# Strassen-like products in the first layer of the last two experts of a balanced mixture, on one core

## The chip, the cores and the metric

The kernel runs on one core of a Trainium2 chip. A core has a matrix engine (TensorE, PE in the profile; its weight loads are shown as PEld), a vector engine (VectorE, DVE), a scalar engine (ScalarE, ACT), a general engine (GpSimd, POOL) and a synchronising engine that starts transfers (SyncE, SP). The metric is the time of one execution on the device in microseconds (us), as the median of several runs.

## What is computed

A linear attention (RWKV-5) over 4 batches, 8 heads, 768 steps and a head dimension of 48 gives 3072 rows of 384 channels. These go through a mixture of 8 experts, which each take exactly 384 tokens, chosen by sorted gate values:

```python
def _moe_ref(x, w_gate, w1, w2) -> np.ndarray:        # N, D, E, F = 3072, 384, 8, 1024
    cap = N // E                                      # 384 tokens of each expert
    logits = x @ w_gate
    ...                                               # greedy, balanced assignment of tokens to experts
    for e in range(E):
        mask = assigned == e
        h = np.maximum(x[mask] @ w1[e], 0.0)          # first layer: 384 x 384 by 384 x 1024
        out[mask] = h @ w2[e]                         # second layer: 384 x 1024 by 1024 x 384
```

Everything is float32. The change concerns the line of the first layer, for the two experts that the kernel takes last.

## The kernel before

The experts are taken one after the other, n = 0 to 7. For each of them the kernel knows the 384 tokens by then, has gathered their rows into `xg` and loaded the weights; it turns the rows to `xT` (channels on the partitions), computes the first layer into `hid`, and the second layer into the output's rows. Constants: `KD = 3` blocks of 128 channels, `KF = 8` blocks of 128 hidden units, `CAP = 384` tokens, `NC = 3` blocks of 128 tokens, `HF = 4`, `HX = 192`.

The first layer is straight: eight blocks of hidden units by three blocks of channels, so 24 matmuls of 384 columns.

```python
    def products(h_ps, j, w1, xT, cols=slice(0, CAP)):
        for f in range(KD):
            product = nc.tensor.matmul(h_ps[:, cols], w1[:, f, ts(j, 128)], xT[:, f, cols],
                                       start=(f == 0), stop=(f == KD - 1))
        return product.ins

    def hidden(hid, j, w1, xT):
        h_ps = ps_h.tile([128, CAP], F32, name="h_ps")
        product = products(h_ps, j, w1, xT)
        nc.scalar.activation(hid[:, j, :], h_ps, AF.Relu)
        return product
```

The second layer is straight for the last block of 128 tokens (`result`, 8 matmuls of 384 columns). For the first two blocks together (`results`) it already uses seven products of sums of quarters instead of eight: the quarters of `hid` (two blocks of tokens by two halves of the hidden units) and of `w2` (two halves of the hidden units by two halves of the channels). The sums are made on VectorE, of `w2` in `halves_of`, of `hid` in `S`:

```python
    def halves_of(w2):
        B = [[w2[:, ts(i, HF), ts(j, HX)] for j in range(2)] for i in range(2)]
        T = [tpool.tile([128, HF, HX], F32, name=f"T{i}") for i in range(4)]
        for t, a, b in ((0, B[0][1], B[0][0]), (1, B[1][1], T[0]), (2, B[1][1], B[0][1]), (3, B[1][0], T[1])):
            nc.vector.tensor_sub(T[t], a, b)
        return B, T

    def results(n, hid, weights, tok, turn):
        B, T = weights
        A = [[hid[:, ts(k, HF), ts(c, 128)] for k in range(2)] for c in range(2)]
        S = ...                                       # 4 sums of 128 x 512 on VectorE
        ...
        p1, p6 = pair((A[0][0], B[0][0]), (S[1], T[1]))     # a pair: 2 x 4 matmuls of 192 columns
        one = spool.tile([128, HX], F32, name="one")
        nc.scalar.copy(one, p1)
        both = sum_of(p6, one, "both")
        p7, p5 = pair((S[2], T[2]), (S[0], T[0]))
        low = sum_of(p7, both, "low")
        nc.vector.tensor_add(out[1][:, HX:DX], p5, low)
        high = sum_of(p5, both, "high")
        xT = turn()                                   # transposes of the next expert's rows
        p2, p4 = pair((A[0][1], B[1][0]), (A[1][1], T[3]))
        ...
        p3, = pair((S[3], B[1][1]))
        nc.vector.tensor_add(out[0][:, HX:DX], p3, high)
        store(n, 0, out[0], tok)
        return xT, added[-1]
```

The loop: while one expert is computed, `following` finds the next expert's tokens and starts the loads of its weights. For most experts that is a search with matmuls and many small VectorE operations; for the last expert only the remaining tokens have to be listed (`walk.remainder`).

```python
        else:                                         # n = 1 to 7
            ...
                weights_2 = halves_of(at["w2"])
            walk.behind = hidden(hid, 0, at["w1"], xT)
            if n + 1 < E:
                ahead = following(n + 2 == E)
            for j in range(1, KF):
                hidden(hid, j, at["w1"], xT)
            for _ in result(n, 2, hid, at["w2"], at["tok"]):
                pass
        xT, added = results(n, hid, weights_2, at["tok"], lambda: turn(ahead["xg"]) if n + 1 < E else None)
```

The accumulators lie in PSUM: two buffers `h_ps`, two buffers `o_ps` and two for transposes, each in a bank of its own. `w1`, `w2`, `T`, `S` and the sums have two buffers each. The order of instructions on each engine isn't that of the text: a scheduler lays it out by the order of the text and by when it reckons that operands are ready, so that a later operation may be put into a gap ahead of an earlier one.

Of the kernel before, what the change touches and what calls it, by code (L numbers as in the profile page):

```python
# [11 lines left out]
F32 = mybir.dt.float32  # L12
# [4 lines left out]
AF = mybir.ActivationFunctionType  # L17
# [5 lines left out]
T = 128  # L23
# [1161 lines left out]
def rwkv5_eagle_then_base_layer_balanced(  # L1185
# [12 lines left out]
    nc = tc.nc  # L1198
    N, DX = out.shape
    E, _, F = moe_w1.shape  # L1200
    NT = N // 128
    CAP = N // E
    NC = CAP // 128
    KD = DX // 128
    KF = F // 128
# [10 lines left out]
    def ask(number, w1, cols=slice(0, F)):  # L1216

        def by(fmax):
            nc.vector.tensor_scalar(out=number, in0=fmax[0:1, :], scalar1=-1.0, scalar2=float(E),
                                    op0=ALU.mult, op1=ALU.add)  # L1220
            weights(number, w1, cols, nc.sync)
        return by
# [8 lines left out]
    def fetch(xg):  # L1231
        def rows(tok):
            for c in range(NC):
                nc.gpsimd.indirect_dma_start(  # L1234
                    out=xg[:, c, :], out_offset=None, in_=x_dram,
                    in_offset=bass.IndirectOffsetOnAxis(ap=tok[:, c:c + 1], axis=0))
        return rows
# [4 lines left out]
    xg = once.tile([128, NC, DX], F32, name="xg")  # L1242
    w1 = once.tile([128, KD, F], F32, name="w1")
    ahead = dict(walk.slots(), number=number, w1=w1, xg=xg)
# [29 lines left out]
    spool = ctx.enter_context(tc.tile_pool(name="f_s", bufs=2))  # L1274
    opool = ctx.enter_context(tc.tile_pool(name="f_o", bufs=3))
    ps_t = ctx.enter_context(tc.tile_pool(name="f_ps_t", bufs=2, space=PSUM))
    ps_h = ctx.enter_context(tc.tile_pool(name="f_ps_h", bufs=2, space=PSUM))
    ps_o = ctx.enter_context(tc.tile_pool(name="f_ps_o", bufs=2, space=PSUM))

    def second(at, queue):  # L1280
        if "w2" not in at:
            at["w2"] = wpool.tile([128, KF, DX], F32, name="w2")
        w2 = at["w2"]
        queue.dma_start(w2, moe_w2[which(at["number"], queue)].rearrange("o (c p) d -> p (o c) d", p=128))

    def following(last, pieces=None, late=None):
        at = dict(walk.slots(), number=xpool.tile([1, 1], I32, name="number"),
                  w1=wpool.tile([128, KD, F], F32, name="w1"), xg=xpool.tile([128, NC, DX], F32, name="xg"))
        make = at, ask(at["number"], at["w1"]), fetch(at["xg"])
        if last:  # L1290
            walk.remainder(*make)
        else:
            if pieces:

                def between(most):
                    for _ in range(most):
                        next(pieces, None)

                with tc.manual_schedule(engines={nc.tensor.engine}):
                    next(pieces)  # L1300
                    walk.between = between
                    listed = walk.search(at)
                    walk.between = Assignment.between
                    for _ in pieces:
                        pass
                with tc.issue_after(listed):
                    late()
            else:
                walk.search(at)
            walk.settle(*make)  # L1310
        second(at, nc.sync)
        return at

    def turn_rows(xT, xg, c):
        xT_ps = ps_t.tile([128, KD, 128], F32, name="xT_ps")
        for f in range(KD):
            nc.tensor.transpose(xT_ps[:, f, :], xg[:, c, ts(f, 128)], ident)  # L1317
        return nc.scalar.copy(xT[:, :, ts(c, 128)], xT_ps).ins  # L1318

    def turn(xg):  # L1320
        xT = xpool.tile([128, KD, CAP], F32, name="xT")
        for c in range(NC):
            turn_rows(xT, xg, c)
        return xT
# [7 lines left out]
# [5 lines that stand above are left out]
# [27 lines left out]
            nc.scalar.activation(hid[:, j, :], h_ps, AF.Relu)  # L1364
            yield

    HF, HX = KF // 2, DX // 2

    def halves_of(w2):

# [6 lines that stand above are left out]
    def store(n, c, o_sb, tok):  # L1377
        nc.gpsimd.indirect_dma_start(  # L1378
            out=out_rows[n * NC + c], out_offset=bass.IndirectOffsetOnAxis(ap=tok[:, c:c + 1], axis=0),
            in_=o_sb, in_offset=None)  # L1380

    def result(n, c, hid, w2, tok):

        o_ps = ps_o.tile([128, DX], F32, name="o_ps")
        for j in range(KF):
            nc.tensor.matmul(o_ps, hid[:, j, ts(c, 128)], w2[:, j, :], start=(j == 0), stop=(j == KF - 1))  # L1386
            yield
        o_sb = opool.tile([128, DX], F32, name="o_sb")
        nc.scalar.copy(o_sb, o_ps)
        store(n, c, o_sb, tok)  # L1390
# [5 lines that stand above are left out]
        S = [spool.tile([128, HF, 128], F32, name=f"S{i}") for i in range(4)]  # L1396
        nc.vector.tensor_sub(S[2], A[0][0], A[1][0])
        nc.vector.tensor_add(S[0], A[1][0], A[1][1])
        nc.vector.tensor_sub(S[1], S[0], A[0][0])
        nc.vector.tensor_sub(S[3], A[0][1], S[1])  # L1400

        def pair(*factors):
            o_ps = ps_o.tile([128, DX], F32, name="o_ps")
            parts = [o_ps[:, ts(i, HX)] for i in range(len(factors))]
            for part, (a, b) in zip(parts, factors):
                for j in range(HF):
                    nc.tensor.matmul(part, a[:, j, :], b[:, j, :], start=(j == 0), stop=(j == HF - 1))  # L1407
            return parts

        def sum_of(product, other, name):  # L1410
            out = spool.tile([128, HX], F32, name=name)
            added.append(nc.vector.tensor_add(out, product, other).ins)  # L1412
            return out

        added = []
        out = [opool.tile([128, DX], F32, name="o_sb") for _ in range(2)]
        p1, p6 = pair((A[0][0], B[0][0]), (S[1], T[1]))
# [7 lines that stand above are left out]
        xT = turn()  # L1425
        p2, p4 = pair((A[0][1], B[1][0]), (A[1][1], T[3]))
        nc.vector.tensor_add(out[1][:, 0:HX], p4, low)  # L1427
        store(n, 1, out[1], tok)
        nc.vector.tensor_add(out[0][:, 0:HX], p2, one)  # L1429
# [5 lines that stand above are left out]
    for n in range(E):  # L1435
        at = ahead
        hid = hpool.tile([128, KF, CAP], F32, name="hid")
        if n == 0:
            xT = xpool.tile([128, KD, CAP], F32, name="xT")
            at["w2"] = wpool.tile([128, KF, DX], F32, name="w2")  # L1440
            weights_2 = []

            def late():
                weights_2[:] = halves_of(at["w2"])

            ahead = following(n + 2 == E, chain(opening(hid, at, xT), result(n, 2, hid, at["w2"], at["tok"])), late)
        else:
            with ExitStack() as order:
                if n == 1:

                    order.enter_context(tc.issue_after(added))
                weights_2 = halves_of(at["w2"])
            walk.behind = hidden(hid, 0, at["w1"], xT)
            if n + 1 < E:
                ahead = following(n + 2 == E)
            for j in range(1, KF):
                hidden(hid, j, at["w1"], xT)
            for _ in result(n, 2, hid, at["w2"], at["tok"]):
                pass
        xT, added = results(n, hid, weights_2, at["tok"], lambda: turn(ahead["xg"]) if n + 1 < E else None)  # L1460


# [26 lines left out]
```

## Time and profile before

| | before |
|---|---|
| time, median of 3 runs | 407.87 us (407.75 to 408.34) |
| span of the profiled execution | 406.8 us |
| first layer of expert 6 on the chain, with the list of the last tokens | 338.78 to 354.75 us |
| first layer of expert 7 on the chain | 370.13 to 385.62 us |
| w1 of expert 6 asked for | 319.10 us |
| w2 of expert 6, w1 of expert 7 asked for | 326.44 and 327.90 us |
| w2 of expert 7 asked for | 338.81 us |

Times in the trace count from the start of the span. A line of the groups gives the line of the kernel, the engine, the operation, its output and inputs, the shape and how often it occurs; then, behind the first bar, the busy time in us and the mean of one in ns, and behind the second the time that the engine stood idle just before such operations, and for whom it waited. A line of the chain gives the start, the length and what ran. Matmuls of float32 show as two records each. Their durations overlap in the trace, so that what one costs in a stream is the time of a stretch of the chain divided by the records in it. In the kernel before, L1328 is the first layer, L1386 the straight part of the second, L1407 its seven products, L1374 the differences of w2, L1397 to L1400 the sums S, L1412 the sums of products, L1317 and L1318 the turning of the rows.

### The profile page before, as it was taken

What the parts mean: (1) busy time and instruction counts of PE and PEld (TensorE: products, weight loads), DVE (VectorE), ACT (ScalarE), POOL (GpSimd) and SP (SyncE); (2) the same over time, 40 slices, a digit from 0 to 9 for tenths busy, and PEclk for the clock granted to TensorE, in tenths of its full rate; (3) what the DMA queues carried; (4) which work ended last, traced back from release to release, by engine and by line L of the source; (5) the groups of instructions that cost most, each with busy time, mean ns of one, the idle gap of its engine ahead of it and who ended that gap; (6) DMA issues with size and microseconds to landing.
All of it is one profiled execution on the core that took longest, in us unless ns stands there. A gap on an engine that the chain in (4) does not pass through costs nothing. (4 is left out here: it accounts for less than half of the span.)

```text
span 406.8 us, 8488 instructions
## 1 busy us (share of the span) xinstructions
PE 391.7 (96%) x3178; PEld 289.9 (71%) x3178; DVE 263.7 (65%) x768; ACT 147.2 (36%) x378; POOL 118.9 (29%) x154
## 2 busy tenths in 40 slices
PE   6999999999998899999999999999999999999993
PEld 3788888888876585865775785695596586587582
DVE  6998879877668268678478568757666836420021
ACT  3897877878756031212112112112121121211200
POOL 5855865656100302220320320320202022301001
PEclk9999999999999999999999999999999999999998
DMA  7989998720039564613711810731551497201001
GB/s 150 200 156 192 190 186 162 147 53 2 3 125 342 146 234 169 220 39 135 255 40 45 294 70 21 250 140 39 186 204 39 157 322 254 65 21 39 0 21 39
DMA packets 93996, 54.43 MB, mean 134 GB/s; under 512 B 76784, under 2 KB 88176, under 8 KB 93936
## 3 DMA queue, kind: packets, MB, share of 16 engines
q1 hardware_dynamic: 89280, 41.70, 37.3%
q0 software_dynamic: 3072, 9.44, 7.1%
q10 hardware_dynamic: 1584, 2.56, 1.9%
q8 instruction: 29, 0.48, 0.5%
q14 instruction: 31, 0.25, 0.2%
HBM read 44.25 MB, written 9.44 MB: 132 GB/s over the span
## 5 line engine op out<-in xcount | busy, mean ns | idle before, releaser
L1328 PE MATMUL h_ps<-xT,w 128*128 128x384 f32 (+1 forms) x372 | 121.7, 475 | 0.0
L1328 PEld LDWEIGHTS h_ps<-xT,w 128*128 128x128 f32 x372 | 64.6, 190 | 35.9 <-issue 4.0
L1335 ACT ACTIVATE hid<-h_ps 128x384 f32<-128x384 f32 x56 | 27.5, 491 | 113.4 <-PE h_ps L1328 100.0
L1234 POOL DMA_INDIRECT xg<-x_rows,tok x24 | 25.0, 1042 | 143.0 <-issue 97.9
L451 ACT ACTIVATE AT<-ident,dd 128x128 f32<-128x128 f32 x188 | 58.1, 393 | 0.0
L1378 POOL DMA_INDIRECT out_dram<-o_sb,tok x24 | 27.9, 1163 | 102.4 <-DVE o_sb L1429 62.9
L1386 PE MATMUL o_ps<-w,hid 128*128 128x384 f32 x128 | 44.4, 493 | 0.9
L521 DVE COPY_PREDICATED AT<-mask,g_ps 128x512 f32<-128x512 uint8 x48 | 32.5, 730 | 6.7 <-PE g_ps L519 6.6
L1386 PEld LDWEIGHTS o_ps<-w,hid 128*128 128x128 f32 x128 | 23.5, 190 | 18.5 <-issue 4.4
L1407 PE MATMUL o_ps<-T,S 128*128 128x192 f32 x192 | 32.5, 326 | 0.0
L1407 PEld LDWEIGHTS o_ps<-T,S 128*128 128x128 f32 x192 | 31.4, 190 | 0.0
L519 PE MATMUL g_ps<-rT,kT 48*128 48x128 f32 x384 | 28.0, 285 | 0.0
L442 POOL TENSOR_TENSOR rk<-rk,u_bc 128x384 f32<-128x384 f32 x24 | 26.8, 1118 | 1.9
L441 POOL TENSOR_TENSOR rk<-rt,kt 128x384 f32<-128x384 f32 x24 | 25.1, 1045 | 6.0 <-DVE AT L521 3.5
L519 PEld LDWEIGHTS g_ps<-rT,kT 48*128 48x128 f32 x384 | 23.4, 187 | 4.0 <-issue 3.2
L564 PE MATMUL y_ps<-AT,vt 128*64 128x128 f32 x368 | 24.6, 276 | 0.0
L1407 PE MATMUL o_ps<-w,hid 128*128 128x192 f32 x128 | 24.6, 326 | 0.0
L1318 ACT COPY xT<-xT_ps 128x384 f32<-128x384 f32 x24 | 10.8, 481 | 34.7 <-PE xT_ps L1317 34.7
L1407 PEld LDWEIGHTS o_ps<-w,hid 128*128 128x128 f32 x128 | 20.9, 190 | 2.1
L463 DVE TENSOR_TENSOR rT<-rT_ps,wr 128x512 f32<-128x512 f32 x24 | 16.5, 687 | 7.6 <-PE rT_ps L458 7.4
L564 PEld LDWEIGHTS y_ps<-AT,vt 128*64 128x64 f32 x368 | 19.7, 137 | 0.9 <-issue 0.3
L1412 DVE TENSOR_TENSOR both<-o_ps,one 128x192 f32<-128x192 f32 x8 | 2.9, 358 | 25.0 <-ACT one L1419 25.0
(236 smaller groups left out, 592.2 us busy)
## 6 DMA issues: line engine op xcount, KB each, us to landing
w<-in_moe_w_dram SPq DMA_DIRECT2D x14, 1536.0 KB, 7.3
kt<-in_k_dram SPq DMA_DIRECT2D x24, 192.0 KB, 3.8
rt<-in_r_dram SPq DMA_DIRECT2D x24, 192.0 KB, 4.0
vt<-in_v_dram SPq DMA_DIRECT2D x24, 192.0 KB, 3.7
x_rows<-AT SPq DMA_DIRECT2D x8, 192.0 KB, 2.3
w<-in_moe_w_dram ACTq DMA_DIRECT2D x1, 1536.0 KB, 9.1
x_rows<-rt SPq DMA_DIRECT2D x6, 192.0 KB, 2.1
x_rows<-ks SPq DMA_DIRECT2D x5, 192.0 KB, 2.2
```

Source lines behind the costliest of these rows:

```text
L441: nc.gpsimd.tensor_mul(rk, rt[:, :, 0:D], kt)
L442: nc.gpsimd.tensor_mul(rk, rk, self.u_bc.rearrange("p (h d) -> p h d", h=H))
L451: self.tc.nc.scalar.activation(AT[:, h % 2, h // 2, :], self.ident, AF.Copy, scale=dd[:, h:h + 1])
L519: nc.tensor.matmul(g_pss[q][:, a, :], kT[heads[q], a, :], rT[heads[q], a, :], start=True, stop=True)
L521: nc.vector.copy_predicated(out=AT[:, q], mask=mask.unsqueeze(1).to_broadcast([128, HP, T]), data=g_pss[q])
L564: nc.tensor.matmul(y[j][halves[i], g, :], vt[:, 2 * a + j, :], AT[:, j, a, :], start=(c == 0 and g == 0), stop=(g == 1), skip_group_check= ...
L1234: nc.gpsimd.indirect_dma_start(out=xg[:, c, :], out_offset=None, in_=x_dram, in_offset=bass.IndirectOffsetOnAxis(ap=tok[:, c:c + 1], axis=0))
L1328: product = nc.tensor.matmul(h_ps[:, cols], w1[:, f, ts(j, 128)], xT[:, f, cols], start=(f == 0), stop=(f == KD - 1))
L1335: nc.scalar.activation(hid[:, j, :], h_ps, AF.Relu)
L1378: nc.gpsimd.indirect_dma_start(out=out_rows[n * NC + c], out_offset=bass.IndirectOffsetOnAxis(ap=tok[:, c:c + 1], axis=0), in_=o_sb, in_of ...
L1386: nc.tensor.matmul(o_ps, hid[:, j, ts(c, 128)], w2[:, j, :], start=(j == 0), stop=(j == KF - 1))
L1407: nc.tensor.matmul(part, a[:, j, :], b[:, j, :], start=(j == 0), stop=(j == HF - 1))
```

## The change

Experts 6 and 7 compute their first layer with seven products of sums of quarters instead of eight, for the first two of the three blocks of channels; the third block is added straight, into the same accumulators. The quarters of w1 are two blocks of channels by two halves of the hidden units, those of x two blocks of channels by two halves of the tokens (192 columns). The work goes in two groups g of two blocks of hidden units each. Its purpose is to give TensorE fewer columns to stream, for sums on VectorE, which has little to do beside these two experts. The sums of w1 (`halves_of_first`) are asked for inside the second layer of the expert before; the differences of w2 for the second layer (`halves_of`) after the first group instead of ahead of the first layer. For expert 6 the list of the last tokens is asked for ahead of the whole first layer instead of after its first block.

```diff
+    def halves_of_first(w1):
+        A = [[w1[:, k, ts(i, F // 2)] for k in range(KD)] for i in range(2)]
+        S = [spool.tile([128, HF, 128], F32, name=f"S{i}").rearrange("p j f -> p (j f)") for i in range(4)]
+        nc.vector.tensor_add(S[0], A[1][0], A[1][1])
+        nc.vector.tensor_sub(S[1], S[0], A[0][0])
+        nc.vector.tensor_sub(S[2], A[0][0], A[1][0])
+        nc.vector.tensor_sub(S[3], A[0][1], S[1])
+        return A, S
+
+    def hidden_by_sums(hid, weights, xT, meanwhile):
+        A, S = weights
+        B = [[xT[:, k, ts(j, HC)] for j in range(2)] for k in range(KD)]
+        T = [spool.tile([128, HC], F32, name=f"x{i}") for i in range(5)]
+        for t, a, b in ((0, B[0][1], B[0][0]), (1, B[1][1], T[0]), (2, B[1][1], B[0][1]), (3, B[1][0], T[1]),
+                        (4, B[2][0], B[2][1])):
+            nc.vector.tensor_sub(T[t], a, b)
+        for g in range(HF // 2):
+            def product(pool, name, *factors):
+                ps = pool.tile([128, CAP], F32, name=name)
+                for q in range(2):
+                    for i, (a, b) in enumerate(factors):
+                        nc.tensor.matmul(ps[:, ts(q, HC)], a[:, ts(2 * g + q, 128)], b,
+                                         start=(i == 0), stop=(i == len(factors) - 1))
+                return ps.rearrange("p (q t) -> p q t", q=2)
 ...                                        # sum_of: an add on VectorE; part: an add on VectorE into hid, then a relu
+            p1 = product(ps_h, "h_ps", (A[0][0], B[0][0]))
+            one = spool.tile([128, 2, HC], F32, name="one_1")
+            nc.scalar.copy(one, p1)
+            p2 = product(ps_h, "h_ps", (A[0][1], B[1][0]), (A[0][2], B[2][0]))
+            part(0, 0, p2, one)
+            p6 = product(ps_o, "o_ps", (S[1], T[1]))
+            both = sum_of(p6, one, "both_1")
+            p7 = product(ps_o, "o_ps", (S[2], T[2]), (A[1][2], B[2][1]))
+            low = sum_of(p7, both, "low_1")
+            p5 = product(ps_h, "h_ps", (S[0], T[0]))
+            part(1, 1, p5, low)
+            high = sum_of(p5, both, "high_1")
+            p3 = product(ps_h, "h_ps", (S[3], B[1][1]), (A[0][2], B[2][1]))
+            part(0, 1, p3, high)
+            p4 = product(ps_o, "o_ps", (A[1][1], T[3]), (A[1][2], T[4]))
+            part(1, 0, p4, low)
+            if g == 0:
+                meanwhile()
 ...
-        else:
+        elif n + 2 < E:
 ...                                        # experts 1 to 5 as before
+        else:
+            if n + 1 < E:
+                ahead = following(True)
+            weights_2 = []
+            hidden_by_sums(hid, weights_1, xT, lambda: weights_2.extend(halves_of(at["w2"])))
+            for _ in result(n, 2, hid, at["w2"], at["tok"]):
+                pass
+
+        def coming():
+            if n + 1 == E:
+                return None, None
+            return turn(ahead["xg"]), halves_of_first(ahead["w1"]) if n + 3 >= E else None
+
+        (xT, weights_1), added = results(n, hid, weights_2, at["tok"], coming)
```

More of the change, by code (lines that the diff above doesn't have):

```diff
@@ L1365, in opening @@
             yield
-    HF, HX = KF // 2, DX // 2
+    HF, HX, HC = KF // 2, DX // 2, CAP // 2
+    def halves_of_first(w1):
[6 more added lines that the diff above has]
+        return A, S
@@ new lines, in hidden_by_sums, with sum_of, part @@
+    def hidden_by_sums(hid, weights, xT, meanwhile):
[13 more added lines that the diff above has]
+                return ps.rearrange("p (q t) -> p q t", q=2)
+            def sum_of(product, other, name):
+                out = spool.tile([128, 2, HC], F32, name=name)
+                nc.vector.tensor_add(out, product, other)
+                return out
+            def part(i, j, product, other):
+                out = hid[:, i * HF + 2 * g:i * HF + 2 * g + 2, ts(j, HC)]
+                nc.vector.tensor_add(out, product, other)
+                nc.scalar.activation(out, out, AF.Relu)
+            p1 = product(ps_h, "h_ps", (A[0][0], B[0][0]))
[16 more added lines that the diff above has]
+                meanwhile()
@@ L1453, in rwkv5_eagle_then_base_layer_balanced @@
             walk.behind = hidden(hid, 0, at["w1"], xT)
-            if n + 1 < E:
-                ahead = following(n + 2 == E)
+            ahead = following(False)
             for j in range(1, KF):
@@ L1459, in rwkv5_eagle_then_base_layer_balanced @@
                 pass
-        xT, added = results(n, hid, weights_2, at["tok"], lambda: turn(ahead["xg"]) if n + 1 < E else None)
+        else:
[10 more added lines that the diff above has]
+        (xT, weights_1), added = results(n, hid, weights_2, at["tok"], coming)
 _INS = ['r', 'k', 'v', 'w', 'u', 'moe_w_gate', 'moe_w1', 'moe_w2']
```

## The prediction

> **What bounds the kernel now.** I read the engine totals first, then the chain of work that ended last, then busy time by stretch for the last experts, and last the groups of instructions by shape. The totals:
>
> ```profile
> PE 391.7 (96%) x3178; PEld 289.9 (71%) x3178; DVE 263.7 (65%) x768; ACT 147.2 (36%) x378; POOL 118.9 (29%) x154
> ```
>
> PE is busy all the time, but its ends are modelled, so the chain has to confirm it. In order of time (start us, us, what), the chain over the last two experts:
>
> ```profile
> 338.78 1.94 PE h_ps L1328 x6
> ...
> 340.76 3.96 PE h_ps L1328 x12
> ...
> 345.62 9.13 PE h_ps L1328 x28
> 354.75 5.16 PE o_ps L1386 x16
> 359.91 5.20 PE o_ps L1407 x32
> ...
> 370.13 15.48 PE h_ps L1328 x48
> 385.62 5.16 PE o_ps L1386 x16
> 390.77 7.81 PE o_ps L1407 x48
> ```
>
> Here the reader sees that TensorE never waits for another engine from 338.8 to 398.6 us, and what one record costs in a stream. Each matmul of float32 shows as two records (24 matmuls of the last first layer, 48 records). 15.48 / 48 = **322.5 ns for 384 columns**; 5.20 / 32 = 7.81 / 48 = **162.6 ns for 192 columns**. These spacings count, not the durations of the groups (495 and 326 ns below), which overlap. At 192 columns only 162.6 x 2 - 322.5 = 2.7 ns per pair are lost: halving the width is almost free, although each of the narrow matmuls needs its own weight load.
>
> ```profile
> L1328 PE MATMUL h_ps<-xT,w 128*128 128x384 f32 x336 | 116.9, 495 | 0.0
> L1407 PE MATMUL o_ps<-T,S 128*128 128x192 f32 x192 | 32.5, 326 | 0.0
> L1374 DVE TENSOR_TENSOR T<-w 128x768 f32<-128x768 f32 x16 | 14.7, 952 | 3.1 <-DMA w<-in_moe_w_dram 3.1
> L873 DVE TENSOR_TENSOR ind<-m,cand 128x384 bf16<-128x384 f32 x21 | 11.7, 556 | 0.5
> L1399 DVE TENSOR_TENSOR S<-S,hid 128x512 f32<-128x512 f32 x8 | 5.7, 707 | 0.2
> L1412 DVE TENSOR_TENSOR both<-o_ps,one 128x192 f32<-128x192 f32 x8 | 2.9, 358 | 25.0 <-ACT one L1419 25.0
> ```
>
> The question is then whether VectorE has room. Busy time by stretch, for the first layers of expert 5, 6 and 7 (stretch and length, then PE, PEld, DVE, ACT, POOL; clock; DMA):
>
> ```profile
> 307.40:322.80 15.40, 15.40 (x66) 8.54 (x64) 11.69 (x49) 3.44 (x7) 0.97 (x1) 1.00 0.23 75
> 338.80:354.75 15.95, 15.95 (x58) 9.22 (x58) 8.44 (x22) 3.44 (x7) 5.10 (x5) 1.00 0.50 160
> 370.13:385.62 15.49, 15.49 (x50) 9.13 (x49) 1.05 (x2) 3.44 (x7) 1.33 (x2) 1.00 0.07 25
> ```
>
> VectorE is busy 11.69 of 15.40 us beside expert 5, where a whole search for the next tokens runs, 8.44 of 15.95 beside expert 6 and 1.05 of 15.49 beside expert 7. That is why only the last two are changed. The clock is 1.00 throughout.
>
> [...]
>
> **The change part by part.**
>
> *Removed, on the path:* for each of experts 6 and 7, 24 matmuls of 384 columns, 48 x 322.5 = 15.48 us.
>
> *Added, on the path:* for each of two groups g, products with one pair of factors (p1, p6, p5) take 2 matmuls and those with two (p2, p7, p3, p4) take 4: 3 x 2 + 4 x 4 = 22, for both groups 44 matmuls of 192 columns, 88 records: 88 x 162.6 = 14.31 us. The straight form would be 48 such matmuls; one eighth is saved on two thirds of the channels, so a twelfth. **Gain: 15.48 - 14.31 = 1.17 us per expert, 2.34 us for both.**
>
> *Added, beside it, on VectorE, per expert:* four sums of w1's quarters of 128x512, 4 x 0.70 = 2.8 us; five differences of x's halves of 128x192, 5 x 0.36 = 1.8 us; and seven sums of 128x384 per group, 14 x 0.56 = 7.8 us. Together 12.4 us. On ScalarE the eight relus of 384 columns stay, though of other pieces, and two copies of p1 come on top: 2 x 0.48 us. Nothing of the DMA changes.
>
> *Where the 12.4 us lie.* The sums of w1 can run in the second layer of the expert before, once w1 has landed: expert 6's w1 is issued at 319.10 us and takes about 7.3 us, so it is there at 326.4, and VectorE is idle from 327.3 to 331.5 waiting for `both`. The differences of x need the last copy of xT, which ends at 335.72, or 367.07 for expert 7, 3.1 us before the first layer begins; they need 1.8. So when p1 starts its inputs are ready; p6, the first product on a sum, comes 4 + 8 records = 1.95 us later. What stays inside the first layer is 7.8 us of 14.3, evenly spread, plus what was already there.
>
> *Does a product wait for its bank?* I walk one group with 0.65 us for a single product, 1.30 for a double, 0.2 us from PE's end to VectorE's start (as in 368.67 to 368.87 at the end of the second layer), 0.56 per sum. From the start: p1 ends at 0.65, p2 1.95, p6 2.60, p7 3.90, p5 4.55, p3 5.85, p4 7.15. p5 reuses p1's bank at 3.90: its copy is done by 1.35. p3 reuses p2's at 4.55: part 0,0 is done by 2.7. p4 reuses p6's at 5.85: `both` is done by 3.4. The next group's p1 reuses p5's at 7.15: low 4.66, part 1,1 5.3, high 5.9. Its p2 needs p3's bank at 7.8: done by 6.6. Its p7 needs p4's bank at 9.75: done by 7.9. The least slack is 1.2 us. So VectorE doesn't bind by itself, and a single foreign operation of up to about 0.95 us in between is absorbed.
>
> *What can spoil it:* four differences of w2, 4 x 0.95 = 3.8 us, are asked for after the first group. Put in one row, they delay the second group's part 0,0 from 9.9 to about 12.1, against 11.7 when p3 wants its bank: about 0.5 us. For expert 7 the kernel before does them as soon as w2 is there, at 346.7 to 351.1, inside expert 6; then expert 7 is free of them, but expert 6 has them beside its own sums and beside some 3.4 us of small operations for the last tokens (8.4 - 1.3 - 3.8). For expert 6 the load is then 8.4 - 1.3 + 7.8 = about 14.9 us in 14.3 (the 1.3 are its first S sum, 0.7, which can come later, and what expert 5 left over, 0.6). That is more than full, so that a difference or two must slip into the 5.2 us after it, where VectorE has room. I allow **0.4 us of stalls in expert 6 and 0.1 us in expert 7**.
>
> *Sum:* 407.87 - 2.34 + 0.5 = **406.0 us**. The second layers (5.16 + 7.81 us) and the tail after PE stay as they are.
>
> **The rivals.**
> *First: VectorE becomes the bound of expert 6.* For it: the 14.9 us for 14.3, operations that go in order, and a difference of w2 that stands in the queue waiting for its transfer; before, VectorE stood 1.31 us for that transfer (346.69), and sums queued behind it would hold banks. Against it: slack of 1.2 us everywhere and room right after. It would take up to 1.5 us more: about 407.3, hardly a gain.
> *Second: the extra weight loads bind.* 44 loads replace 24, and each takes 190 ns as a record against a spacing of 162.6. For it: 190 is more than 162.6. Against it: the second layer already runs 48 such records in 7.81 us with loads of 190 ns, so they overlap. Were it true, 88 x 190 = 16.7 us, and the time would be 407.9 + 2 x 1.2 = 410.3.
> *Third: no stall at all*, or a changed order around the last tokens' list that also saves some switching: 405.4.
>
> **Range and chances.** The first-order gain is fixed by a count and a measured spacing, so 405.4 is the best case. Stalls decide the rest: 0 to 0.3 us is about as likely as 0.3 to 1.2. The low end is 405.2 (spread of the measurement), the high end 407.3. The third rival has some 30%, the first 15%, the second 2%. 2% of the time is 8.2 us, which neither gain nor loss reaches: faster by over 2% 0.01, within 2% 0.98, slower 0.01.
>
> **What would show it.** In the profile after, the first layer of expert 7 should show 88 records of 192 columns in 14.3 to 14.5 us in the chain, and that of expert 6 in 14.3 to 14.9, where it now has 15.5 and 15.97 with the list's matmuls. VectorE should have 4 x 0.70, 5 x 0.36 and 14 x 0.56 us more per expert, the w1 sums ahead of the first layer. TensorE idling before p3 or p7 of the second group, released by VectorE, would be the first rival. A spacing of 190 ns would be the second. The prediction is wrong if the second layer of expert 5 or 6 grows, because the w1 sums got ahead of `both` and `low`, which I take to keep their times.

## The result and the profile after

The changed kernel takes **405.83 us** (405.41 to 405.93, 6 runs) against 408.00 before (407.75 to 408.54, 6 runs): a ratio of 0.9943, 95% interval 0.9930 to 0.9956. The engine totals of the page after:

```profile
PE 389.7 (96%) x3258; PEld 300.7 (74%) x3258; DVE 284.6 (70%) x814; ACT 149.3 (37%) x382; POOL 120.3 (30%) x154
```

VectorE is busy 20.9 us more than before (284.6 - 263.7), TensorE 2.0 us less. The chain that ended last still runs over TensorE alone from expert 6's first layer on (start us, us, what; L1392 is the new first layer, L1442 the straight part of the second, L1463 its seven products):

```profile
338.51 2.04 PE h_ps L1392 x12
...
346.70 1.40 PE h_ps L1392 x8
...
352.00 1.30 PE o_ps L1392 x8
353.30 5.16 PE o_ps L1442 x16
...
368.68 1.95 PE h_ps L1392 x12
...
381.68 1.30 PE o_ps L1392 x8
382.98 5.16 PE o_ps L1442 x16
388.14 7.81 PE o_ps L1463 x48
```

Expert 7's first layer now lasts from 368.68 to 382.98, 14.30 us for 88 records, 162.5 ns each. Expert 6's, with the list of the last tokens, lasts from 338.46 to 353.30, 14.84 us where it was 15.97. So the chain shows a gain of 1.18 + 1.13 = 2.31 us. TensorE ends 2.63 us earlier in this trace (395.96 against 398.59); the other 0.32 us lie ahead of expert 6's first layer. The second layer of expert 6 keeps its length, 15.38 us from 354.75 before and from 353.30 now: the sums of w1 in it cost TensorE nothing. Busy time in these two stretches (stretch and length, then PE, PEld, DVE, ACT, POOL; clock; DMA):

```profile
338.46:353.30 14.84, 14.84 (x98) 14.65 (x97) 14.52 (x35) 4.00 (x8) 5.93 (x5) 1.00 0.50 160
368.68:382.98 14.30, 14.30 (x90) 14.30 (x89) 7.53 (x15) 4.50 (x9) 1.33 (x2) 1.00 0.08 29
```

The reader sees VectorE at 14.52 of 14.84 us beside expert 6, all but full, and yet TensorE busy in every microsecond of both. No wait of TensorE is left in either stretch. How that goes together, VectorE's timeline in expert 6's second group shows (start us, us, engine, line, operation, output<-inputs):

```profile
346.85 0.95 DVE L1430 TENSOR_TENSOR T<-w 128x768 f32<-128x768 f32 x1
...
347.79 0.95 DVE L1430 TENSOR_TENSOR T<-w 128x768 f32<-128x768 f32 x1
348.65 0.55 DVE L1403 TENSOR_TENSOR hid<-h_ps,one 128x384 f32<-128x384 f32 x1
349.12 0.55 DVE L1398 TENSOR_TENSOR both<-o_ps,one 128x384 f32<-128x384 f32 x1
349.58 0.95 DVE L1430 TENSOR_TENSOR T<-w,T 128x768 f32<-128x768 f32 x1
350.45 0.55 DVE L1398 TENSOR_TENSOR low<-o_ps,both 128x384 f32<-128x384 f32 x1
```

The differences of expert 7's w2 (L1430) don't stand in one row: two lie ahead of the group's first sum, whose product is only then being computed, the others between sums. Each delays a sum by at most about one operation of 0.95 us, less than the slack of a bank, 1.2 us by the walk in the prediction (an estimate); what doesn't fit, the group's last sum, runs from 353.38 to 353.93 us, beside the second layer.

### The profile page after: what moved, and what is told of

Its sections match the earlier page's. It is cut to its first block, busy times and chain, and to the rows that moved or that the text cites. A ratio compares the mean times of both kernels' runs of the same rounds, so it can differ in the third digit from the quotient of the medians.

```text
span 404.2 us, 8713 instructions
## 1 busy us (share of the span) xinstructions
PE 389.7 (96%) x3258; PEld 300.7 (74%) x3258; DVE 284.6 (70%) x814; ACT 149.3 (37%) x382; POOL 120.3 (30%) x154
## 5 line engine op out<-in xcount | busy, mean ns | idle before, releaser
L1328 PE MATMUL h_ps<-xT,w 128*128 128x384 f32 (+1 forms) x276 | 89.9, 470 | 0.0
L1328 PEld LDWEIGHTS h_ps<-xT,w 128*128 128x128 f32 x276 | 46.7, 190 | 24.5 <-issue 4.0
L1335 ACT ACTIVATE hid<-h_ps 128x384 f32<-128x384 f32 x40 | 19.6, 490 | 82.7 <-PE h_ps L1328 74.3
L1442 PE MATMUL o_ps<-w,hid 128*128 128x384 f32 x128 | 44.4, 493 | 0.9
L1442 PEld LDWEIGHTS o_ps<-w,hid 128*128 128x128 f32 x128 | 23.4, 190 | 17.9 <-issue 4.4
L1463 PE MATMUL o_ps<-T,S 128*128 128x192 f32 x192 | 32.5, 326 | 0.0
L1463 PEld LDWEIGHTS o_ps<-T,S 128*128 128x128 f32 x192 | 31.4, 190 | 0.0
L1463 PE MATMUL o_ps<-w,hid 128*128 128x192 f32 x128 | 24.6, 326 | 0.0
L1463 PEld LDWEIGHTS o_ps<-w,hid 128*128 128x128 f32 x128 | 20.9, 190 | 2.1
L431 DVE TENSOR_TENSOR ks<-kt,wk 128x384 f32<-128x384 f32 x24 | 18.9, 787 | 0.0
```

## The experiments

All ratios are to the kernel before, run on the same chip. All differences from the changed kernel below are between such ratios, times 408 us.

### 1. The order without the sums

```diff
-            hidden_by_sums(hid, weights_1, xT, lambda: weights_2.extend(halves_of(at["w2"])))
+            for j in range(KF):
+                hidden(hid, j, at["w1"], xT)
+                if j == 3:
+                    weights_2.extend(halves_of(at["w2"]))
...
-            return turn(ahead["xg"]), halves_of_first(ahead["w1"]) if n + 3 >= E else None
+            return turn(ahead["xg"]), None
```

> Straight first layer for experts 6 and 7 again (24 matmuls of 384 columns each), but the new order kept: the list of the last tokens ahead of expert 6's first layer, the differences of w2 after half of it, no sums. If the gain is TensorE's records times their spacing (my theory), nothing is left of it: 407.9 to 408.2 us, ratio 1.000 +- 0.001, first layers of 15.5 and 15.7 to 16.0 us on the chain. If the gain comes from the new order (rival), it stays near 405.8 us.

Measured: 408.93 us, ratio 1.0017 (1.0003 to 1.0031). The chain has the old first layers again; expert 7's:

```profile
369.88 15.48 PE h_ps L1328 x48
```

Nothing of the gain is left, so the order is not its cause. The 0.2% above the kernel before are not explained: from expert 6's first layer to TensorE's end the trace takes 59.81 us (338.52 to 398.33) as before (338.78 to 398.59), and on this chip both kernels' runs spread up to 410.77 us.

### 2. Only the last expert

```diff
-        elif n + 2 < E:
+        elif n + 1 < E:
...
-            ahead = following(False)
+            ahead = following(n + 2 == E)
...
-            return turn(ahead["xg"]), halves_of_first(ahead["w1"]) if n + 3 >= E else None
+            return turn(ahead["xg"]), halves_of_first(ahead["w1"]) if n + 2 >= E else None
```

> Only expert 7 by seven products, expert 6 straight and in the old order. My theory: half of the gain, 408.0 - 1.17 = 406.8 us, first layer of expert 7 14.3 us and of expert 6 15.97 us as before. If expert 6 gained nothing, because VectorE was nearly full beside it (rival), the whole gain would be here: 405.8 us.

Measured: ratio 0.9972 (0.9955 to 0.9988), 1.1 us less than before, half of the gain. On the chain expert 7's first layer takes 14.29 us (370.04 to 384.33) and expert 6's 15.97 (338.68 to 354.65). So each expert brings its own share of about 1.17 us, and expert 6, with its full VectorE, gains as much as expert 7.

### 3. Each sum with a product twice

```diff
-                nc.vector.tensor_add(out, product, other)
+                for _ in range(2):
+                    nc.vector.tensor_add(out, product, other)
```

(in `sum_of` and in `part`; the second writes the same values again)

> Each of the 14 sums with a product per expert is done twice, so 7.8 us more of VectorE per expert, TensorE's work unchanged. By the load of VectorE that the changed kernel shows beside each first layer: expert 7 has 7.5 + 7.8 = 15.3 us for 14.3, so some 1 to 1.5 us longer; expert 6 has 14.5 + 7.8 = 22.3 us for 14.8, of which 3.8 can slip behind, so some 3.5 us longer; together 410 to 411 us, with TensorE idle before products whose bank VectorE still holds. If there is ample room (the slack of 1.2 us per bank swallows a second sum of 0.56), nothing changes: 405.8 us.

Measured: 413.06 us, ratio 1.0102 (1.0071 to 1.0134), 6.5 us above the changed kernel. Now VectorE binds in expert 6. TensorE's own timeline shows it, and then busy times by stretch (clock is the third number from the end):

```profile
349.18 1.16 PE L1392 MATMUL h_ps<-xT,w 128*128 128x192 f32 x4 [0.87 <-DVE high L1399]
```

```profile
347.00:349.00 2.00, 0.51 (x3) 0.13 (x2) 2.00 (x7) 0.52 (x1) 0.00 (x0) 1.00 0.00 0
...
350.00:351.00 1.00, 1.00 (x5) 1.00 (x4) 1.00 (x3) 0.70 (x2) 0.97 (x1) 0.50 0.00 0
```

The second group's p1 waits for `high`, which still holds its bank, as the walk in the prediction has it. In the two microseconds before, TensorE is busy for 0.51 us and VectorE for all 2.00. Then comes a cost that I had not counted: the granted clock falls to 0.50, where two records take 0.64 us (350.14 to 350.78) instead of 0.325. The 18 records from 349.18 to 354.05 take 4.87 us on the chain instead of 18 x 0.1625 = 2.93, **1.9 us lost to the clock**. Expert 6 waits elsewhere too, 0.80 us for the list of the last tokens, 0.30 us for a copy of xT and 0.62 us in the second layer; expert 7 waits 0.56 us for `high` and 0.38 us in its second layer, somewhat less than the 1 to 1.5 us that I expected there. My expectation of 4.2 to 5.2 us in all was short by about what the clock took.

### 4. Columns of 96

```diff
-                for j in range(KF):
-                    hidden(hid, j, at["w1"], xT)
+                for j in range(KF):                  # expert 7 only, straight
+                    h_ps = ps_h.tile([128, CAP], F32, name="h_ps")
+                    for c in range(CAP // 96):
+                        products(h_ps, j, at["w1"], xT, ts(c, 96))
+                    nc.scalar.activation(hid[:, j, :], h_ps, AF.Relu)
...                                                  # after the fourth block the differences of w2; no sums of w1
```

(against the straight first layer; expert 6 as in the changed kernel)

> Expert 7's first layer straight, but in matmuls of 96 columns: 96 matmuls with 96 weight loads, 192 records; expert 6 by seven products. [...] If the weight load binds below some width, a record takes longer: 190 ns (a load's length in the trace) would make 36.5 us, in all 428 us[...].

Measured: 413.09 us, ratio 1.0105 (1.0073 to 1.0137). The chain has

```profile
368.69 21.41 PE h_ps L1328 x192
```

so 111.5 ns per record. The spacings at 384 and 192 columns, carried on in a straight line, would give 82.5 (an estimate: 162.5 - (322.5 - 162.5) / 2), so here more than the number of columns counts. It is less than the record of a load, 192 ns in this stream, and the time is far below the 428 us that a load's record for each would make. Expert 0's first layer, in the changed kernel's trace, has matmuls of 128 columns with a weight load each:

```profile
145.03 1.50 PE L1328 MATMUL o_ps<-xT,w 128*128 128x128 f32 x12
146.37 0.25 PE L885 MATMUL counts<-prop,ind 128*128 128x64 bf16 x3
```

From 145.03 to 146.37 these 12 records take 111.7 ns each, as much as at 96 columns. So the spacing didn't fall from 128 to 96 columns. That the weight load holds it there is my guess; no run changes the load. The 162.5 ns of 192 columns lie above it. The rival of the extra loads could by this bind only below some 131 columns, an estimate from the three spacings: 192 - (162.5 - 111.5) x 192 / (322.5 - 162.5). A second level of halving, 96 columns, would lose: two such records take 223.0 ns where one of 192 columns takes 162.5, and seven eighths of them would still be 195 (an estimate).

### 5. Expert 5 too

```diff
-        elif n + 2 < E:
+        elif n + 3 < E:
...
-                ahead = following(True)
+                ahead = following(n + 2 == E)
...
-            return turn(ahead["xg"]), halves_of_first(ahead["w1"]) if n + 3 >= E else None
+            return turn(ahead["xg"]), halves_of_first(ahead["w1"]) if n + 4 >= E else None
```

> Expert 5 by seven products too, written as for expert 6. TensorE's count alone (rival) gives a third gain of 1.17 us: 408.0 - 3.5 = 404.7 us. My theory says VectorE has no room there: 11.7 us beside the straight first layer of expert 5 plus 7.8 of sums are 19.5 us for 14.3, and the search for the next tokens, a chain of small operations on VectorE and TensorE, stretches by the sums put between; the rows of expert 6 come later and TensorE waits. 407 to 410 us, slower than the changed kernel.

Measured: 412.46 us, ratio 1.0110 (1.0093 to 1.0127), 6.8 us above the changed kernel and above my range too. But the first layer itself is not where it is lost: in it TensorE is busy for 15.10 of 15.10 us (305.5 to 320.6), search included. The loss comes after it. From the timeline of the changed kernel, the list of expert 6's tokens:

```profile
322.92 0.17 DVE L1181 TENSOR_REDUCE tok<-mine 128x3 int32<-128x12 f32 x1
```

From that of this run, the list and the first transposes of the last of their rows, then TensorE's busy time in the stretch between, and the last row transfer on the chain:

```profile
327.63 0.17 DVE L1181 TENSOR_REDUCE tok<-mine 128x3 int32<-128x12 f32 x1
...
338.14 0.87 PE L1317 MATMUL xT_ps<-ident,xg 128*128 128x128 f32 x3 [3.79 <-DMA xg<-x_rows,tok]
```

```profile
334.00:338.00 4.00, 0.36 (x3) 0.06 (x1) 1.43 (x5) 0.48 (x1) 0.00 (x0) 0.71 0.92 336
```

```profile
331.13 6.88 DMA xg<-x_rows,tok
```

The sums between the search's small operations push the list 4.7 us later, and the rows arrive when TensorE has run out of other work: it waits 1.31 us for the first rows and 3.79 us for the last, and is busy for 0.36 us of four. The longer wait is not owed to the list alone. The last row transfer takes 6.9 us; 1.5 MB of w2 had been asked for 0.2 us before it, at 330.93. The first two, asked for ahead of w2, took 4.3 and 3.5 us. In the changed kernel the last one takes 6.5 us likewise, asked for 0.3 us behind w2, but lands at 332.93, under cover. After the pause the clock is 0.50 again (from 338 to 342 us), and 22 records take 5.35 us (339.02 to 344.37) instead of 3.58. Expert 6's first layer starts at 344.41, 5.9 us later than the changed kernel's.

### 6. The search asked for after two products

```diff
+            if g == 0 and begin:                      # for expert 5; the call of following ahead of the layer falls away
+                begin(latest)                         # walk.behind = the last matmul of p2; ahead = following(False)
             part(0, 0, p2, one)
```

> As the run with three experts, but the search is asked for after the first two products, so that TensorE has work ahead of the search's first matmuls. If the loss there comes from VectorE's load (my theory), it changes little: 407 to 410 us. If it comes from the order on TensorE at the start of the layer (rival), it falls to 404.7 to 405.5 us.

Measured: 409.62 us (407.83 to 412.07), ratio 1.0030 (1.0016 to 1.0043). Still no gain, though better than the run before: the list comes even later (329.27 us), but the wait for expert 6's rows is 1.2 us instead of 5.1. Its three transfers were all asked for before w2 (at 333.92), and the last of them takes less than half the time:

```profile
332.78 3.04 DMA xg<-x_rows,tok
```

With 3.04 us the last rows of the run before would have landed at 334.2 instead of 338.0 us (an estimate from these two lines), so by this most of its wait was what the transfer behind w2 took longer, which the late list had laid bare, and not the late list by itself. Another wait took its place: the transposes of expert 7's first rows were queued among expert 6's products and TensorE stood 2.33 us for those rows. The order decides the size of the loss: my theory expected that it would change little, the rival that the loss would go, and it about halved.

### 7. Sums of weights on GpSimd

```diff
-        nc.vector.tensor_add(S[0], A[1][0], A[1][1])
+        nc.gpsimd.tensor_add(S[0], A[1][0], A[1][1])
 ...                                                  # the other three sums of w1 likewise
-            nc.vector.tensor_sub(T[t], a, b)
+            on.tensor_sub(T[t], a, b)                # expert 5's differences of w2: on = nc.gpsimd
```

> Three experts with the late search, and the sums of w1 for all three and the differences of w2 for expert 5 on GpSimd. VectorE beside expert 5 then has 11.7 - 2.9 (about three of the differences of w2) + 7.8 = 16.6 us for 14.3 plus the 5.2 after it. If VectorE's load is the cause (my theory), most of the loss goes: 405 to 407 us. If the search's chain is long because the sums stand between its operations, whatever the total load, little changes: 407 to 410 us.

Measured: 411.07 us, ratio 1.0088 (1.0055 to 1.0121). Worse than without GpSimd, and above both of my ranges. Its timeline at the start of expert 5's first layer:

```profile
305.29 3.80 POOL L1434 TENSOR_TENSOR T<-w,T 128x768 f32<-128x768 f32 x2
305.46 1.96 DVE L1387 TENSOR_TENSOR x<-xT,x 128x192 f32<-128x192 f32 x1
307.35 1.96 DVE L1387 TENSOR_TENSOR x<-xT 128x192 f32<-128x192 f32 x1
309.23 0.34 DVE L1387 TENSOR_TENSOR x<-xT,x 128x192 f32<-128x192 f32 x1
```

A difference of x takes 0.34 us alone and 1.96 us while GpSimd forms a difference; why, no run shows. So the offload doesn't take load from VectorE here, it holds it up: in 15.10 us of expert 5's first layer (305.5 to 320.6) VectorE gets through 37 operations in 13.92 us busy, where run 5 had 50 in 14.47, and TensorE is busy for 13.21 us instead of 15.10. The list is done only at 331.81 us. The rows, again all asked for ahead of w2, cost TensorE 1.6 us.

### 8. Experts 1 to 7

The run before, with every expert from 1 on by seven products.

```diff
-        elif n + 3 < E:
+        elif n < 1:
...                                                  # and the sums of w1 for every next expert
```

> Experts 1 to 7 by seven products, with the offload of the run before. By TensorE's count alone 7 x 1.17 = 8.2 us: 399.8 us. My theory: each of experts 1 to 5 loses to VectorE and the search's chain what it loses in the three-expert run, so that five times its difference from the changed kernel comes out: from 402 us if that run gains 0.8 us to 420 us if it loses 3.

Measured: 449.56 us, ratio 1.1027 (1.0988 to 1.1066), far above my range. About half of the 44 us above the changed kernel has a name: the holding up by GpSimd falls on the search, and TensorE stands 21.5 us in four places for one small operation of it, of 0.29 us in the median, which takes up to 5.59 us. The first line shows it at 217.76, beside GpSimd's differences of w2, the last at its longest:

```profile
217.76 5.58 DVE L873 TENSOR_TENSOR wide<-digit_of,cnt 128x128 f16<-128x128 f32 x1
217.88 3.56 POOL L1434 TENSOR_TENSOR T<-w 128x768 f32<-128x768 f32 x2
```

```profile
259.78 5.59 DVE L873 TENSOR_TENSOR wide<-digit_of,cnt 128x128 f16<-128x128 f32 x1
```

### 9. Half of expert 5

```diff
+        elif n + 2 < E:                              # n = 5: blocks 0, 1, 4, 5 straight, then group 1 by sums
+            ...
+            walk.behind = hidden(hid, 0, at["w1"], xT)
+            ahead = following(False)
+            for j in (1, HF, HF + 1):
+                hidden(hid, j, at["w1"], xT)
+            hidden_by_sums(hid, weights_1, xT, lambda: None, (1,))
...                                                  # the sums of expert 5's w1 for the second group alone
```

> Experts 6 and 7 as in the changed kernel; expert 5 computes hidden blocks 0, 1, 4, 5 straight and only the second group by seven products, after them: 0.58 us less for TensorE, 3.9 us of sums with products on VectorE instead of 7.8, late in the layer, when most of the search is done. If what matters is how late the list of expert 6's tokens is (my theory: the row `tok` at 327.6 us in the run with three experts against 322.9 in the changed kernel cost the wait for the rows), a list up to some 3 us later is hidden: 405.2 us, 0.6 better than the changed kernel. If VectorE's load alone decides (11.7 + 3.9 = 15.6 us for 15), it is 406 to 408 us.

Measured: 407.85 us (407.27 to 411.67), ratio 1.0003 (0.9992 to 1.0013), 2.4 us above the changed kernel. The profile is of the slowest of these executions (411.67 us), and 2.05 us of its delay lie far ahead of expert 5: the transposes of expert 1's rows stand at 171.52 us, in the changed kernel at 169.47. The list stands at 328.43 us; less these 2.05 it is 3.5 us later than in the changed kernel. Run 5 has 5.0 by the same reckoning, as those transposes stand at 169.14 there. So half the sums do make the list less late, as I expected, but the rows are not hidden: the second and third transfer were asked for at 330.67 and 331.94, behind w2 at 329.97, the second takes 7.0 us, and again TensorE waits for the rows:

```profile
337.77 0.52 PE L1317 MATMUL xT_ps<-ident,xg 128*128 128x128 f32 x3 [2.38 <-DMA xg<-x_rows,tok]
```

In expert 5's first layer TensorE is busy all of the time and VectorE 13.89 of 16.22 us (307.76 to 323.98). This speaks for the time at which the rows come, and not for the sum of VectorE's load, as what decides in expert 5. How long the wait is in an execution of the median time, no profile shows.

### 10. Half of experts 1 to 5

```diff
-        elif n + 2 < E and n < 5:
+        elif n + 2 < E and n < 1:                    # the branch of run 9 from expert 1 on
```

> The same for experts 1 to 5. If the list stays early enough in all of them: 405.8 - 5 x 0.58 = 402.9 us. If in each the list is a little too late and TensorE waits for rows: above 408 us.

Measured: 419.68 us, ratio 1.0313 (1.0268 to 1.0358). The loss repeats from expert to expert: the transposes of the rows of experts 3, 4, 5 and 6 fall ever further behind those of the changed kernel, by 1.4, 3.4, 8.8 and 10.7 us at their first ones. In the waits of TensorE those for the next rows lead, with 5.2 us in six places; 4.7 us more ahead of transposes have no releaser in the profile.

### 11. Three more sums in expert 6

```diff
-                nc.vector.tensor_add(out, product, other)
+                for _ in range(2 if n + 2 == E and g == 1 else 1):
+                    nc.vector.tensor_add(out, product, other)
```

(in `sum_of`)

> As the changed kernel, but in expert 6's second group the sums both, low and high are done twice: 3 x 0.56 = 1.7 us more of VectorE, which was busy 14.52 of 14.84 us there. If the banks' slack of about 1.2 us swallows a sum more each and the differences of w2 slip into the second layer (the walk of my prediction), nothing changes: 405.8 us +- 0.3. If VectorE was full (rival), TensorE waits 1 to 1.7 us: 406.8 to 407.5 us.

Measured: 405.58 us (405.48 to 405.69), ratio 0.9939 (0.9925 to 0.9952), the changed kernel's 0.9943 within the intervals. VectorE is busy 14.49 of 14.85 us there (338.37 to 353.22), as full as it was, and TensorE all of the time; the 1.7 us more pushed the end of the group's last sum from 353.93 to 355.49 us, beside the second layer. So a VectorE at 98% was not a limit yet: run 3, with 7.8 us more in each expert, found it. TensorE's order changed with it: the transposes of expert 7's rows begin at 353.05 instead of 363.50 us, among the second layer's matmuls. Some of the room may come from that; no run holds the order fixed.

No run beat the changed kernel clear of its interval.

## Why the prediction was right

- **Records times spacing** (predicted gain 2.34 us): right. 88 records in 14.30 us are the 162.5 ns that the second layer had shown, and the two stretches gained 1.18 and 1.13 us; the ratio of the times gives 2.3 us (1.8 to 2.9). The spacing was measured at the two widths that the count needs, 322.5 ns at 384 columns and 162.5 at 192. A straight line through them doesn't hold below: at 96 columns it gives 82.5 where 111.5 were measured, at 128 it gives 109.2 where 111.7 were (run 4). Runs 1 and 2 show that the gain belongs to the matmuls, half of it to each expert.
- **Sums of w1 and differences of x ahead of the layer**: right. The sums take 0.68 us each and ran from 326.23 to 329.03 us, in VectorE's pause ahead of `both`; the differences of x ended at 336.86. One thing that the walk had not seen: the sums of w1 went ahead of the small operations that find the last expert's number, so that its w1 was asked for at 330.03 instead of 327.90 us. It is needed much later, and cost nothing.
- **The walk by banks** (slack of at least 1.2 us): right as far as runs 11 and 3 test it. Run 11's second sums cost no wait, with the reserve on TensorE's order said there; in run 3 the longest wait appears at the product and for the sum that the walk names.
- **0.5 us of stalls**: this term of the sum was mis-sized; it measured zero. I had put the four differences of w2 in one row; two stand between the sums, and VectorE's overflow has the second layer to run in. VectorE's load was counted too high as well: 24.8 us more for both experts, where 20.9 were measured, since neighbouring operations overlap by 0.08 to 0.09 us in the trace (the difference of w2 that starts at 347.79 and takes 0.95 ends after the sum at 348.65 begins). The third rival, no stall at all, is what came: from the 408.00 of the later comparison it stands at 408.00 - 2.34 = 405.7 us, and 405.83 was measured. That the 406.0 of the prediction also lies within 0.2 us is in part luck, as the times before rose by 0.13 us.
- **The rivals**: VectorE as the bound of expert 6 fell with run 11, at this load; the weight loads fell with the spacing of 162.5 ns. In run 4 the spacing stayed at 111.5 ns at 96 columns; that loads bind there is not shown.
- **Why only two experts**: the prediction gave VectorE's load as the reason. That was too simple. The first layer of expert 5 ran without a wait in runs 5 and 9; what breaks is the time at which the next expert's rows arrive. The sums put between the search's operations make the list late, but the longest waits come where the rows are then asked for behind w2: 5.1 us in run 5 and 2.4 in run 9, against 1.2 and 1.6 in runs 6 and 7, whose lists are later still but whose rows go ahead of w2.

What stays open: whether a third expert would gain if its rows always went ahead of w2. Runs 6 and 7 had that order only as a side effect, beside other waits; to ask for w2 after the rows, and to change nothing else, was not tried.

## What to carry to other kernels

Price a narrower matmul by its spacing in a stream on the chain (162.5 ns here), not by the duration of its record (326 ns) or of its weight load (190 ns); where a stage of the same kernel already runs that shape, the number is there. An engine at 98% in a stretch was no bound here while its work had buffers' slack and room right after (run 11); but a chain of small dependent operations on that engine was delayed by the operations put between (the list by 4.7 us in run 5), and what waits for the end of that chain paid, the more so where its transfer fell in behind a large one (6.9 us in run 5, 3.0 ahead of it in run 6). Before work is moved to another engine, time what will run beside it: a difference on VectorE went from 0.34 to 1.96 us beside GpSimd (run 7).

## What the runs showed of the hardware

- Where TensorE had been busy for 0.51 us of 2.0 (run 3), and after single waits of 2.33 and 2.38 us (runs 6 and 9), the granted clock was 0.50 for some 3.4 us (an estimate from its means by stretch, 0.72 over 6 us in runs 6 and 9), and records of 192 columns took 320 instead of 162.5 ns (runs 3 and 6). After a wait of 1.31 us (run 5, to 332.93) and one of 1.89 us (run 7, to 310.25) it was still 1.00.
- Float32 matmuls with a weight load of 128 columns each took 111.5 ns per record at 96 columns (run 4) and 111.7 at 128 (the changed kernel), though the record of the load is 190 to 192 ns long.
- A transfer of 128 rows landed 3.0 us (run 6), 3.5 and 4.3 us (run 5) and 3.1 and 3.2 us (the kernel before) after it was asked for ahead of the 1.5 MB of w2, and 6.4, 6.5 and 6.9 us after, where w2 had been asked for 0.2 to 0.4 us before it (the kernel before, the changed kernel, run 5).
- A difference of 128x192 on VectorE took 1.96 us beside GpSimd differences of 128x768 and 0.34 right after them (run 7); an operation of 128x128 took 5.58 us beside such differences, against 0.29 in the median (run 8).
